# Attention beside a gated dense block: the order of the lead-in, with key projections in half pieces, two query transfers on ScalarE's queue and later weight splits

## The chip, the core and the metric

The kernel runs on one core of a Trainium2 chip. The metric is the device time of one execution in microseconds (us), as a median over several runs. Each engine (TensorE or PE, VectorE or DVE, ScalarE or ACT, GpSimd or POOL, SyncE or SP) takes its own instructions strictly in order and meets the others through semaphores; a DMA transfer is issued from an engine's instruction stream. So the order in which instructions stand on each engine is a large part of what a kernel is.

## What is computed

```
xn = layernorm(x)                                  # x: 2048 x 512
q, k, v = xn @ wq, xn @ wk, xn @ wv                # 32 heads of 16; k and v: one head for all
o = softmax(q k^T / 4) v,   s = o @ wo
h = xn @ w1 + b1,   a = h * tanh(softplus(h))      # 512 -> 1792
out = x + s * silu(a @ w2)
```

## The kernel before

The program is written out completely, engine by engine, by a planner in Python. There are two parts.

**The loop** (lines 1573 to 1620) has 512 steps: 32 groups of query heads ("v", 4 heads of one chunk of 512 rows each; c = chunk) times 16 blocks of 128 keys. A step issues 4 score products e (L1098, of 64 rows of the array each; ScalarE takes the exponential of each, L1100), up to 8 half-height pieces of dense products (`Mm.half`, L120, target `xps`), 4 products m (L1119) whose row maxima VectorE takes (L1123), and 4 products pv of exponentials and values (L1187). The m belong to the next group of heads but one: their maxima, turned and moved into two rows of the query tile, become the exponent's shift. Two half-height products, one in each half of the array, run beside each other. The dense products make groups: 12 for a block of 128 columns of q or of the first dense matrix (m1), 15 or 12 for a block of rows of the second (m2). A group of 15 goes through the loop by fives if the planner sees spare steps when the group begins, else by eights (`begin`, `g.most`).

**The lead-in** (lines 1277 to 1551) computes what the first step needs: statistics and norms of the four chunks of x, their transposition by TensorE (L302, `xp`), the first query projection (12 products), keys and values of all four chunks, and the first 40 pairs of m, a pair being the product for either half of the array and its two maxima. For chunks 1 to 3 the keys and values go four stages: `k_part` (`kq`, 16 products of 32 output rows, L336), a copy by ScalarE (`k_stage`, `vt`), `k_sum` (`kp`, one product, L345), and copies into `ks` by ScalarE (`k_high`, L356) and then VectorE (`k_low`, L239). A pair m_n of head group 0 needs the keys of chunk n/8. Values follow through `vt`, a transposition by TensorE (`vp`, L372) and a copy by VectorE into `vaug` (L375).

The lead-in's order is made by a list scheduler over `Task` objects (engine, planned duration, function, dependencies, a priority). At each turn it takes the option with the earliest planned start. If TensorE has a gap longer than a bound, option "X" puts three dense products into it (`fill(3)`) or a filler (`keep_warm`, target `warm`, L1434); if ScalarE has one, option "J" splits a weight (float32 into a high part by ScalarE, L461, and a low part by GpSimd, L164) or runs a piece of the activation of m1 (`hb`, `t`, `u`). The maxima use three banks of PSUM (six once the last transposition is issued), so a product m waits for the maximum three products earlier. The evacuation of a finished dense group is a task for ScalarE, not before 0.35 us (2.9 us for the first query group) after the group's end (`put_off`).

The first query group's result (`qh`, `ql`) goes into the query tiles of head groups 0 and 1 by 24 transfers of 32 KB (L784), 12 for each, all from SyncE's queue: piece p (pairs m_0 to m_3 need p = 0, m_4 to m_7 p = 1) and half a, each with two copies of `qh` and one of `ql`. `q_dma` makes the tasks for it.

Of the kernel before, what the change touches and what calls it, by code (L numbers as in the profile page):

```python
# [126 lines left out]
def block_kernel(ctx: ExitStack, tc: tile.TileContext, x, wq, wk, wv, wo, w1, b1, w2, out):  # L127
# [200 lines left out]
    kq_of = {}  # L328
    vp_of = {}

    def k_part(c):
        kq = ps_v.tile([P, C], F32, tag="v", name=f"kq{c}")
        for h in range(2):
            z = slice(C // 2 * h, C // 2 * (h + 1))
            for dt in range(NDT):
                pe.matmul(kq[32 * dt:32 * dt + 32, z], wkf[:, dt, P - 32:P], xf_of[c][dt // 2][:, dt % 2, z], start=True, stop=True)  # L336
        kq_of[c] = kq
# [420 lines left out]
    def q_group(c, b):  # L758
        it = item("wq", ("q", b), wq[:, P * b:P * (b + 1)].rearrange("(t p) n -> p t n", p=P))

        def post(ps):
            qh = sb.tile([P, C], F32R, tag="qh", name=f"qh{c}_{b}", bufs=1)
            ql = sb.tile([P, C], F32R, tag="ql", name=f"ql{c}_{b}", bufs=1)
            first = (c, b) == (0, 0)
            if first:
                act.activation(qh, ps, AF.Copy)
                lead["q"](lambda: sub(dve, ql, ps, f(qh)))
            else:
                qf = sb.tile([P, C], F32, tag="qf", name=f"qf{c}_{b}", bufs=1)
                act.activation(qf, ps, AF.Copy)  # L770
                gap[0] += 1
                hi_pool(qh, qf)
                sub(pool, ql, qf, f(qh))
            for k in range(2):
                v = 8 * c + 2 * b + k

                def dmas(v=v, k=k, parts=((0, 0), (0, 1), (1, 0), (1, 1))):
                    q = qt_of[v] = qts[v % 3]
                    for p, a in parts:
                        o = 64 * a  # L780
                        r = 64 * k + 16 * (2 * p + a)
                        for d, src in ((o, qh), (o + 16, qh), (o + 32, ql)):
                            sp_at(0.63)
                            sp.dma_start(f(q[d:d + 16, p]), f(src[r:r + 16]))  # L784
                if first:
                    lead["qdma"](lambda ps, dmas=dmas: dmas(parts=[(p, a) for p in ps for a in range(2)]))
# [538 lines left out]

    def q_dma(fn):
        v = len(qready)
        qready[v] = None

        def move(p):  # L1330
            fn(ps=(p,))
            qready[v] = (qready[v] or ()) + (now[0] + 6 * 0.63 + 2.0,)
        for p in range(2):
            task("SP", 6 * 0.63, lambda p=p: move(p), [lead["qlow"]], prio=1 + p + 2 * v)

    lead["q"], lead["qdma"] = q_low, q_dma

# [28 lines left out]
    for c0, c1 in ((0, 1), (1, 2), (2, 3), (3, 4)):  # L1366
# [4 lines left out]
        for c in range(c0, c1):  # L1371
# [39 lines left out]
            if c == 0:  # L1411
                k0 = kp = task("PE", 0.9, lambda c=c: k_proj(c, (0,)), xs)
                for dt in range(1, 4):
                    kp = task("PE", 0.9, lambda c=c, dt=dt: k_proj(c, (dt,)), [kp], lat=0.0)
            else:
                kq = task("PE", 1.0, lambda c=c: k_part(c), xs)
                kg = task("ACT", 0.6, lambda c=c: k_stage(c), [kq])
                bank("v", 1, kq, [kg])
                k0 = kp = task("PE", 1.0, lambda c=c: k_sum(c), [kg])
# [38 lines left out]
    while True:  # L1458
# [27 lines left out]
        if k == "M":  # L1486
            if MSEQ[m_next[0]] == (0, 8 * NC - 8):
                keep_warm(3)
            for a in range(2):
                m_one(a)  # L1490
            d = max(T["DVE"], s + 0.45)
            m_ends += [d + 0.6, d + 1.2]
            T["DVE"] = d + 1.2
            T["PE"] = s + (0.25 if kind[0] == "M" else 0.45)
            kind[0] = "M"
            if vdone[0] == 0 and min(m_next) >= m_need(0):
                vdone[0] = 1
                r = c_rows(0)
                r1 = task("DVE", 0.85, lambda r=r: (r[0](), r[1](), r[2](), r[3]()), prio=-4)
                rows[:] = [r1]  # L1500

                def move():
                    r[4]()
                    cdone[0] = now[0] + 2 * 0.65 + 2.0
                task("SP", 2.6, move, [r1])
        elif k == "X":
            fresh = cur["g"] is None
            if cur["g"] is not None or not waiting and begun[0] < 1 + (s - 18) / X_US and begin():
                begun[0] += fresh
                fill(3)  # L1510
                T["PE"] = s + 0.23 * 3 + (0.2 if kind[0] == "M" else 0)
                kind[0] = "X"
            else:
                keep_warm()
                T["PE"] = s + 0.25
                kind[0] = "X"
        elif k == "J":
            tag = next((g for g in ("wq", "ws", "wb") if (g == "wq" or s > 19.0) and arrived(g) and busy[0] + E0 < s + 0.5), None)
            n = ran[0]
            if tag:  # L1520
                split(tag)
                T["ACT"] = s + 0.6
            else:
                gap[0] = 0
                if not pool_due():
                    act_jobs(1)
                T["ACT"] = s + (0.65 if ran[0] > n else 0.15)
        else:
            plan[e].remove(k)
            k.fn()  # L1530
            T[e] = max(s, T[e]) + k.us + (0.15 if e == "PE" and kind[0] == "M" else 0)
            k.end = T[e]
            if e == "PE":
                kind[0] = "T"
# [102 lines left out]
```

## Time and profile before

| | |
|---|---|
| median of 3 runs (1576.19 to 1576.45) | 1576.33 us |
| the profiled execution | 1576.55 us |
| its span, first to last instruction | 1574.4 us |
| busy: TensorE, VectorE, ScalarE, GpSimd | 1562.6, 1341.1, 1307.8, 633.7 us |
| granted TensorE clock | 1.0 |
| first m product | 24.73 us after the span's start |
| last maxima of head group 0 done, turning begins (L1154) | 72.31 us |
| first half-height product (the loop's first step) | 77.93 us |
| first pv | 86.26 us |

A row of the timeline has start, length, engine, line, operation, output and inputs, shapes and types, a count of merged instructions, and in brackets how long the engine idled before it and what ended the wait. The chain of waits is followed back from the last instruction: at each point it names what was late. A row of the windows has the stretch, its length, and for each engine the busy time with the number of instructions. TensorE is busy 99% of the span, but ends of products are modelled, so its share does not tell how full it is; in the lead-in one reads VectorE's gaps instead.

### The profile page before, as it was taken

To read this page: it belongs to the slowest core of one execution; us is meant where nothing else is said; L and a number is where in the kernel's file an instruction comes from. 1 tells how busy PE (TensorE), PEld (TensorE's weight loads), DVE (VectorE), ACT (ScalarE), POOL (GpSimd) and SP (SyncE) were. 2 spreads that over 40 slices of the span, in tenths; PEclk is the share of its full clock that TensorE was granted. 3 is DMA by queue.
4 is the path that set the end of the run, shared out by engine and by line. 5 is a ranking of instruction groups with operands and counts; after the bars stand their busy time and mean duration, and the time that the engine had idled before them with its cause. 6 is when DMAs were issued, how large, how long until landed. Compare 5 with 4: busy or idle time off the path is not lost.

```text
span 1574.4 us, 31742 instructions
## 1 busy us (share of the span) xinstructions
PE 1562.6 (99%) x11738; PEld 842.0 (53%) x11738; DVE 1341.1 (85%) x2329; ACT 1307.8 (83%) x2518; POOL 633.7 (40%) x683
## 2 busy tenths in 40 slices
PE   9999999999999999999999999999999999999998
PEld 5555555555555555555555555555555555555554
DVE  8998888889889888888998988888889998888832
ACT  7588788798998779878989887887898878789886
POOL 4774266284464105503515320471251515126412
PEclk9999999999999999999999999999999999999999
DMA  6243231232331314122032222211332213032020
GB/s 191 93 124 112 65 101 44 60 118 84 125 97 41 103 44 137 45 69 83 24 100 65 64 93 69 85 59 30 112 99 85 74 40 111 19 111 58 15 81 28
DMA packets 74666, 124.31 MB, mean 79 GB/s; under 512 B 21520, under 2 KB 35344, under 8 KB 74512
## 3 DMA queue, kind: packets, MB, share of 16 engines
q1 hardware_dynamic: 74512, 122.29, 25.2%
q8 instruction: 93, 1.52, 0.4%
q14 instruction: 61, 0.50, 0.1%
HBM read 74.78 MB, written 26.21 MB: 64 GB/s over the span
## 4 chain that ended last, share of the span: by engine, by line
PE 95%; DVE 4%; ACT 1%; DMA 0%; issue 0%; SPq 0%; ACTq 0%; DVEq 0%
PE xps L120 44%; PE pv L1187 32%; PE e L1098 9%; PE m L1119 7%; DVE mb L1123 3%; PE late L120 1%; PE xps L116 0%; ACT pt L1100 0%; DMA xin<-in_dram 0%; PE late L1098 0%; PE kp L351 0%; PE wop L120 0%; PE xp L302 0%; PE late L116 0%; PE wop L116 0%
## 5 line engine op out<-in xcount | busy, mean ns | idle before, releaser
L1123 DVE TENSOR_REDUCE mb<-m 128x1 f32<-128x512 f32 x2048 | 1274.2, 683 | 171.3 <-PE m L1119 152.3
L1100 ACT ACTIVATE pt<-e 128x512 f32<-128x512 f32 x2018 | 1061.6, 602 | 220.7 <-PE e L1098 212.3
L1119 PE MATMUL m<-ks,qt 48*128 48x512 f32 (+1 forms) x2048 | 829.9, 421 | 1.6 <-DVE ks L239 0.5
L1098 PE MATMUL e<-qt,ks 64*128 64x512 f32 x2018 | 740.4, 401 | 0.3
L1187 PE MATMUL pv<-pt,vaug 128*32 128x512 f32 x4096 | 543.0, 604 | 0.0
L1119 PEld LDWEIGHTS m<-ks,qt 48*128 48x128 f32 (+1 forms) x2048 | 372.9, 185 | 55.7 <-DVE mb L1123 18.5
L1098 PEld LDWEIGHTS e<-qt,ks 64*128 64x128 f32 x2018 | 373.3, 186 | 17.9 <-ACT pt L1100 7.5
L120 PE MATMUL xps<-wbs,act 64*128 64x512 f32 x1248 | 339.1, 408 | 0.2
L120 PEld LDWEIGHTS xps<-wbs,act 64*128 64x128 f32 x1248 | 217.7, 185 | 177.4 <-ACT pt L1100 105.8
L120 PE MATMUL xps<-xt,ws 64*128 64x512 f32 x1104 | 305.8, 410 | 0.1
L120 PEld LDWEIGHTS xps<-xt,ws 64*128 64x128 f32 x1104 | 190.6, 185 | 182.7 <-ACT pt L1100 116.5
L174 POOL TENSOR_SCALAR t<-t 128x512 f32<-128x512 f32 x56 | 34.4, 615 | 395.1 <-ACT t L838 394.9
L1187 PEld LDWEIGHTS pv<-pt,vaug 128*32 128x32 f32 x4096 | 81.9, 108 | 137.4 <-issue 129.1
L164 POOL TENSOR_TENSOR hb<-hb,t 128x512 f32<-128x512 f32 x56 | 72.1, 1287 | 65.6 <-ACT t L851 52.4
L120 PE MATMUL xps<-xt,wq 64*128 64x512 f32 x336 | 93.2, 410 | 0.0
L120 PEld LDWEIGHTS xps<-xt,wq 64*128 64x128 f32 x336 | 58.0, 185 | 55.2 <-ACT pt L1100 35.2
L120 PE MATMUL xps<-wbs,ot_all 64*128 64x512 f32 x288 | 79.5, 409 | 0.0
L120 PEld LDWEIGHTS xps<-wbs,ot_all 64*128 64x128 f32 x288 | 49.6, 185 | 46.7 <-ACT pt L1100 29.3
L164 POOL TENSOR_TENSOR hb<-hb,u 128x512 f32<-128x512 f32 x56 | 72.3, 1291 | 4.4
L164 POOL TENSOR_TENSOR u<-u,t 128x512 f32<-128x512 f32 x56 | 71.8, 1282 | 4.7
L164 POOL TENSOR_TENSOR act<-hb,act 128x512 fp32r<-128x512 f32 x55 | 70.8, 1288 | 4.6
L159 POOL TENSOR_SCALAR qh<-qf 128x512 fp32r<-128x512 f32 x15 | 9.3, 620 | 111.8 <-ACT qf L770 76.2
(158 smaller groups left out, 954.9 us busy)
## 6 DMA issues: line engine op xcount, KB each, us to landing
wbs<-w SPq DMA_DIRECT2D x36, 512.0 KB
ws<-w SPq DMA_DIRECT2D x35, 512.0 KB
qt<-qh SPq DMA_DIRECT2D x256, 32.0 KB
w<-wbs SPq DMA_DIRECT2D x14, 512.0 KB
wq<-wq SPq DMA_DIRECT2D x14, 512.0 KB
wbs<-wo SPq DMA_DIRECT2D x12, 512.0 KB
rawws<-in_dram SPq DMA_DIRECT2D x21, 256.0 KB
rawwb<-in_dram SPq DMA_DIRECT2D x20, 256.0 KB
```

The costliest lines, as they stand in the source:

```text
L120: i = self.pe.matmul(ps, self.lhs()[o], self.rhs()[o], start=(self.k == 0 and self.halves == 0), stop=(self.k == self.tot - 1 and self.hal ...
L159: pool.tensor_scalar(o, i, 1.0, 0.0, op0=ALU.mult, op1=ALU.add)
L164: eng.tensor_tensor(out=o, in0=a, in1=b, op=op)
L174: pool.tensor_scalar(o, o, lim, 0.0, op0=ALU.min, op1=ALU.max)
L1098: pe.matmul(e, ks[o:o + 64, P * k:P * (k + 1)], q[o:o + 64, p], start=True, stop=True)
L1100: r = act.activation(pt, e, AF.Exp, scale=0.25)
L1119: pe.matmul(m, q[o, p, P * t:P * (t + 1)], ks[o, C * kb:C * (kb + 1)], start=True, stop=True)
L1123: r = dve.reduce_max(out=mb_of[v][:, kb, z:z + 1], in_=m, axis=AX.X)
L1187: pe.matmul(o[32 * j:32 * j + 32], vaug[:, k], pt, start=(k == 0), stop=(k == 15))
```

## The change

- `k_part` and `k_sum` take a half h of the 512 columns and become two tasks of 0.5 us each instead of one of 1.0, so other work can stand between the halves.
- `q_dma`: of the six transfers for the first piece of head group 0, the two copies of `qh` for half 1 are issued from ScalarE's queue right behind the copy that makes `qh`; SyncE's task for that piece has four left (planned as 3 x 0.63 us). The planned duration of that ScalarE task grows from 0.69 to 1.95 us.
- The task for `ql` gets priority -4.
- Option X is offered for gaps over 0.15 us instead of 0.35.
- A weight split in option J also waits until GpSimd has no task due (norms of chunks 2 and 3).

```
-    def k_part(c):
-        kq = ps_v.tile([P, C], F32, tag="v", name=f"kq{c}")
-        for h in range(2):
+    def k_part(c, h):
+        if not h:
+            kq_of[c] = ps_v.tile([P, C], F32, tag="v", name=f"kq{c}")
+        kq = kq_of[c]
+        for h in (h,):
...
-    def k_sum(c):
-        kp_of[c] = ps_v.tile([P, C], F32, tag="v", name=f"kp{c}")
-        pe.matmul(kp_of[c], ksum, vt_of[c], start=True, stop=True)
+    def k_sum(c, h):
+        if not h:
+            kp_of[c] = ps_v.tile([P, C], F32, tag="v", name=f"kp{c}")
+        z = slice(C // 2 * h, C // 2 * (h + 1))
+        pe.matmul(kp_of[c][:, z], ksum, vt_of[c][:, z], start=True, stop=True)
...
-                        for d, src in ((o, qh), (o + 16, qh), (o + 32, ql)):
-                            sp_at(0.63)
-                            sp.dma_start(f(q[d:d + 16, p]), f(src[r:r + 16]))
+                        for n in which:
+                            if eng is sp:
+                                sp_at(0.63)
+                            eng.dma_start(f(q[o + 16 * n:o + 16 * n + 16, p]), f((qh, qh, ql)[n][r:r + 16]))
...
-        t = task("ACT", 0.69, fn, at=now[0] + lead.get("late", 0.35))
+        t = task("ACT", 1.95 if "late" in lead else 0.69, fn, at=now[0] + lead.get("late", 0.35))
...
-        lead["qlow"] = task("DVE", 0.69, fn, at=T["ACT"] + 0.7)
+        lead["qlow"] = task("DVE", 0.69, fn, at=T["ACT"] + 0.7, prio=-4)
...
-        def move(p):
-            fn(ps=(p,))
-            qready[v] = (qready[v] or ()) + (now[0] + 6 * 0.63 + 2.0,)
+        def move(p, n):
+            if v or p:
+                fn(parts=[(p, 0), (p, 1)])
+            else:
+                fn(parts=[(p, 0)])
+                fn(parts=[(p, 1)], which=(2,))
+            qready[v] = (qready[v] or ()) + (now[0] + n * 0.63 + 2.0,)
+        if not v:
+            fn(parts=[(0, 1)], which=(0, 1), eng=act)
...
-                kq = task("PE", 1.0, lambda c=c: k_part(c), xs)
+                k0 = task("PE", 0.5, lambda c=c: k_part(c, 0), xs)
+                kq = task("PE", 0.5, lambda c=c: k_part(c, 1), [k0], lat=0.0)
...
-        if e0 is None or e0[0] > T["PE"] + 0.35:
+        if e0 is None or e0[0] > T["PE"] + 0.15:
...
-            tag = next((g for g in ("wq", "ws", "wb") if (g == "wq" or s > 19.0) and arrived(g) and busy[0] + E0 < s + 0.5), None)
+            tag = next((g for g in ("wq", "ws", "wb") if (g == "wq" or s > 19.0) and arrived(g) and busy[0] + E0 < s + 0.5 and not pool_due()), None)
```

Since the scheduler decides by planned times, all of the lead-in's order changes, and the loop's up to step 24; from there on TensorE's order is the same as before. Line numbers after the change are larger by up to 13. Three places follow. In the names, the number after m_ is the half of the array and the next one the pair; numbers at the end of a name count tiles.

TensorE, from the last key product of chunk 0 to the second pair of m. Before:

```order
L351 MATMUL kp_323<-xf_1_279,wkf 128x512 x2
L1434 MATMUL warm<-qt_79 128x512 x3
L116 MATMUL xps<-xt_216,ws_341 128x512 x9
L372 MATMUL vp_391<-ident,vt_368 128x32 x4
L302 MATMUL xp_397<-ident,xin_0_164 128x128 x4
L1119 MATMUL m_0_0_407<-ks,qt_77 128x512
L1119 MATMUL m_1_0_410<-ks,qt_77 128x512
L302 MATMUL xp_417<-ident,xin_1_166 128x128 x4
L1119 MATMUL m_0_1_423<-ks,qt_77 128x512
```

And now:

```order
L354 MATMUL kp_327<-xf_1_279,wkf 128x512 x2
L1447 MATMUL warm<-qt_79 128x512 x7
L1123 MATMUL m_0_0_386<-ks,qt_77 128x512
L1123 MATMUL m_1_0_389<-ks,qt_77 128x512
L1447 MATMUL warm<-qt_79 128x512 x3
L375 MATMUL vp_401<-ident,vt_370 128x32 x4
L1123 MATMUL m_0_1_413<-ks,qt_77 128x512
```

Nine dense products have left this place, the first pair stands ahead of the value transposition vp, and fillers and vp stand between the first and the second pair.

VectorE, around the copy into ks for chunk 1 (mb of two numbers: the maxima of head groups 0 and 1). Before:

```order
L1123 TENSOR_REDUCE mb_406<-m_1_7_535 128x1
L239 SCALAR_TENSOR_TENSOR ks<-ks,ksgn,kp_524 112x512
L1123 TENSOR_REDUCE mb_553<-m_0_0_554 128x1
L1123 TENSOR_REDUCE mb_553<-m_1_0_557 128x1
L1123 TENSOR_REDUCE mb_553<-m_0_1_571 128x1
L1123 TENSOR_REDUCE mb_553<-m_1_1_574 128x1
L375 COPY vaug<-vp_565 128x4x16
L1123 TENSOR_REDUCE mb_406<-m_0_8_593 128x1
```

And now:

```order
L1127 TENSOR_REDUCE mb_385<-m_1_7_531 128x1
L1127 TENSOR_REDUCE mb_539<-m_0_0_540 128x1
L1127 TENSOR_REDUCE mb_539<-m_1_0_543 128x1
L1127 TENSOR_REDUCE mb_539<-m_0_1_556 128x1
L1127 TENSOR_REDUCE mb_539<-m_1_1_559 128x1
L239 SCALAR_TENSOR_TENSOR ks<-ks,ksgn,kp_536 112x512
L1127 TENSOR_REDUCE mb_385<-m_0_8_571 128x1
```

The copy has moved behind the two pairs of head group 1 and directly ahead of m_8, the first pair that needs it. The copy for chunk 2 stands directly ahead of m_16 now, where it stood ahead of m_11; that for chunk 3 stands ahead of m_24 in both.

TensorE in the loop, step 20 up to its last e (xps<-wbs,act: the second dense matrix). Before:

```order
L120 MATMUL xps<-wbs,act_1_833 128x512
L1119 MATMUL m_1_16_1924<-ks,qt_79 128x512
L120 MATMUL xps<-wbs,act_2_1094 128x512
L1098 MATMUL e_0_1928<-qt_78,ks 128x512
L120 MATMUL xps<-wbs,act_2_1094 128x512
L1119 MATMUL m_1_17_1933<-ks,qt_79 128x512
L120 MATMUL xps<-wbs,act_2_1094 128x512
L1098 MATMUL e_1_1937<-qt_78,ks 128x512
L120 MATMUL xps<-wbs,act_3_1311 128x512
L1098 MATMUL e_2_1942<-qt_78,ks 128x512
L1119 MATMUL m_0_16_1946<-ks,qt_79 128x512
L1098 MATMUL e_3_1949<-qt_78,ks 128x512
```

And now, from its second e:

```order
L1102 MATMUL e_1_1942<-qt_78,ks 128x512
L120 MATMUL xps<-wbs,act_1_1046 128x512
L1123 MATMUL m_1_18_1947<-ks,qt_79 128x512
L120 MATMUL xps<-wbs,act_1_1046 128x512
L1102 MATMUL e_2_1951<-qt_78,ks 128x512
L120 MATMUL xps<-wbs,act_2_1219 128x512
L1123 MATMUL m_1_19_1956<-ks,qt_79 128x512
L120 MATMUL xps<-wbs,act_2_1219 128x512
L1102 MATMUL e_3_1960<-qt_78,ks 128x512
```

The step holds eight half-height pieces where it held five. Counted over the order, the lead-in issues 66 dense products where it issued 75, and the loop up to the end of step 23 has 144 halves where it had 126.

More of the change, by code (lines that the diff above doesn't have):

```diff
@@ L336, in k_part @@
                 pe.matmul(kq[32 * dt:32 * dt + 32, z], wkf[:, dt, P - 32:P], xf_of[c][dt // 2][:, dt % 2, z], start=True, stop=True)
-        kq_of[c] = kq
     def k_stage(c):
@@ L775, in post, with dmas @@
                 v = 8 * c + 2 * b + k
-                def dmas(v=v, k=k, parts=((0, 0), (0, 1), (1, 0), (1, 1))):
+                def dmas(v=v, k=k, parts=((0, 0), (0, 1), (1, 0), (1, 1)), which=(0, 1, 2), eng=sp):
                     q = qt_of[v] = qts[v % 3]
@@ L781, in dmas @@
                         r = 64 * k + 16 * (2 * p + a)
-                        for d, src in ((o, qh), (o + 16, qh), (o + 32, ql)):
-                            sp_at(0.63)
-                            sp.dma_start(f(q[d:d + 16, p]), f(src[r:r + 16]))
+                        for n in which:
+                            if eng is sp:
+                                sp_at(0.63)
+                            eng.dma_start(f(q[o + 16 * n:o + 16 * n + 16, p]), f((qh, qh, ql)[n][r:r + 16]))
                 if first:
-                    lead["qdma"](lambda ps, dmas=dmas: dmas(parts=[(p, a) for p in ps for a in range(2)]))
+                    lead["qdma"](dmas)
                 else:
@@ L1328, in q_dma @@
         qready[v] = None
-        def move(p):
-            fn(ps=(p,))
-            qready[v] = (qready[v] or ()) + (now[0] + 6 * 0.63 + 2.0,)
+        def move(p, n):
[7 more added lines that the diff above has]
+            fn(parts=[(0, 1)], which=(0, 1), eng=act)
         for p in range(2):
-            task("SP", 6 * 0.63, lambda p=p: move(p), [lead["qlow"]], prio=1 + p + 2 * v)
+            n = 6 if v or p else 3
+            task("SP", n * 0.63, lambda p=p, n=n: move(p, n), [lead["qlow"]], prio=1 + p + 2 * v)
     lead["q"], lead["qdma"] = q_low, q_dma
```

5 lines of the change are left out of this document (3 added, 2 removed).

## The prediction

> **What bounds the kernel now.** I read the page's span first, then the chain of waits over the first 95 us, then VectorE's timeline there. Where the lead-in ends, the chain reads (start, length, what ended last, number of instructions):
>
> ```profile
> 73.25 12.54 DVE mb L1123 x21
> 85.84 0.49 PE m L1119
> ```
>
> The profiled execution took 1576.55 us, 2.15 around its span of 1574.4, and 0.22 more than the median of 1576.33. Up to 85.84 the chain is VectorE's row maxima (L1123); from there TensorE holds it, step after step. So the change, whose new order ends before step 24 of 512, can gain only where VectorE idles before 85.84, and pays where it leaves TensorE more work after that. VectorE's rows, the idle time ahead of a group in brackets:
>
> ```profile
> 22.86 0.75 DVE L239 SCALAR_TENSOR_TENSOR ks<-ks,ksgn,kp 112x512 fp32r<-112x512 f32 x1
> ...
> 25.26 8.89 DVE L1123 TENSOR_REDUCE mb<-m 128x1 f32<-128x512 f32 x14 [0.71 <-PE m L1119]
> 34.42 1.29 DVE L1123 TENSOR_REDUCE mb<-m 128x1 f32<-128x512 f32 x2 [0.27 <-PE m L1119]
> 35.63 0.74 DVE L239 SCALAR_TENSOR_TENSOR ks<-ks,ksgn,kp 112x512 fp32r<-112x512 f32 x1
> 36.28 2.48 DVE L1123 TENSOR_REDUCE mb<-m 128x1 f32<-128x512 f32 x4
> 38.67 0.22 DVE L375 COPY vaug<-vp 128x64 f32<-128x64 f32 x1
> 38.80 1.28 DVE L1123 TENSOR_REDUCE mb<-m 128x1 f32<-128x512 f32 x2
> 41.33 1.29 DVE L1123 TENSOR_REDUCE mb<-m 128x1 f32<-128x512 f32 x2 [1.24 <-PE m L1119]
> ...
> 47.66 13.58 DVE L1123 TENSOR_REDUCE mb<-m 128x1 f32<-128x512 f32 x22
> 61.16 0.74 DVE L239 SCALAR_TENSOR_TENSOR ks<-ks,ksgn,kp 112x512 fp32r<-112x512 f32 x1
> 62.48 2.48 DVE L1123 TENSOR_REDUCE mb<-m 128x1 f32<-128x512 f32 x4 [0.59 <-PE m L1119]
> ...
> 73.17 14.40 DVE L1123 TENSOR_REDUCE mb<-m 128x1 f32<-128x512 f32 x24
> ```
>
> A run of 24 maxima lasts 14.40, so one pitch is 0.60 and a pair (both halves of the heads) 1.20; a copy into ks takes 0.65 of the queue (35.63 to 36.28), a copy into vaug about 0.14 (38.67 to 38.80). From 25.26 to 62.48 there are 52 maxima, 26 pairs. The waits worth having are the 0.27, the 1.24, another between 41.33 and 47.66 (eight maxima and the copies into ks and vaug need 5.6 of those 6.33), short ones inside the first group, the late start at 25.26, and the 0.59 behind the last ks copy. After 47.66 there is little to win but that last one. A chain that starts earlier gains at 62.48 only what it has not lost by then in new waits.
>
> **The first maximum.** TensorE and the transfers ahead of it:
>
> ```profile
> 20.50 1.26 PE L1434 MATMUL warm<-qt 128*128 128x512 f32 x3
> ...
> 24.73 0.49 PE L1119 MATMUL m<-ks,qt 64*128 64x512 f32 x2
> ```
>
> ```profile
> 18.29 1.24 SPq L784 DMA_DIRECT2D qt<-qh  x2
> ...
> 21.46 0.59 SPq L784 DMA_DIRECT2D qt<-ql  x1
> ...
> 24.54 2.25 SPq L784 DMA_DIRECT2D qt<-qh  x2
> ```
>
> The ks copy ends at 23.61; vp and a transposition stand between it and the first score product at 24.73, whose maximum follows 0.53 later. Now the product stands directly behind seven fillers, which start at 20.50 and take 0.3 to 0.4 each: 23.3 at the latest. It waits for ks alone: issue 23.66, maximum 24.19, **1.07 earlier**. Its six query transfers were all issued by 22.05 and had landed by 24.73, so landing takes at most 2.7. With two of them on ScalarE, SyncE issues its four by about 20.8, landed by 23.5 at the latest. The move to ScalarE therefore buys nothing beyond that; ks would be waited for anyway. On ScalarE nothing showed a DMA issue yet. Bounds: nothing, and the longest here, 2.25 for two. I take 1.2 for two as in SyncE's rows: qh ends at 18.27, so ScalarE is free at 19.5, and the first norm (0.45), one sum (0.7) and the first ks (from 21.17, behind its product) follow without delay. At 2.25 ks would still start by about 21.8, some 0.6 late, and VectorE, busy until 22.86, would see nearly nothing of it.
>
> The Trainium skill, page "DMA: Bandwidth & Descriptors", section "Issuing engines are not separate DMA queues", says that such a move saves only the sequencer's time to issue, since all queues share the same DMA engines. By it the move is worth at most the 1.2 of issue and, with ks later than the transfers, 0 in the sum; the trace has the issue time but shows no transfer from ScalarE.
>
> **From the second pair to the fourth chunk's keys.** The price list for what stands between two pairs:
>
> ```profile
> 35.78 0.73 PE L1434 MATMUL warm<-qt 128*128 128x512 f32 x2
> 36.51 0.41 PE L372 MATMUL vp<-ident,vt 32*128 32x32 f32 x4
> ...
> 39.80 1.07 PE L336 MATMUL kq<-xf,wkf 128*32 128x256 f32 x16
> ...
> 43.10 0.96 PE L116 MATMUL xps<-xt,ws 128*128 128x512 f32 x3
> ```
>
> I take 0.75 for three products (their rows overlap the next pair by 0.2), 0.6 for a transposition, 0.55 for half of kq, as much for half of kp, and 0.43 for a pair. So a pair with one of these beside it fits in about 1.2, and kq and kp in one piece no longer hold VectorE up by 1.24. But the new order puts other things between:
> - Second pair: three fillers, the last of which needs the bank of the first maximum (ends 24.85), then vp: product 25.5, maximum 26.03 where VectorE was free at 25.47. **New wait 0.56.**
> - Nine pairs to the second pair of head group 1, one vaug copy and 0.3 of small lateness (where two transpositions, or a half of kq and one, share a gap): 26.03 + 10.8 + 0.14 + 0.3 = 37.3.
> - The second ks copy now comes after those two pairs, at 37.3 to 37.95, and the next product needs it. Before, the same two pairs stood behind it and hid the way over TensorE. **New wait 0.55** (the 0.59 of 62.48 shows such a one): maximum at 38.5, against 38.80.
> - Then 0.43 + 0.75 + two fillers 0.6 + vp 0.37 ahead of the next product: 40.1, maximum 40.65, **wait 0.8**, where it was 1.24.
> - Seven pairs and a vaug copy: 40.65 + 8.4 + 0.15 = 49.2.
> - The third ks copy follows there, again with the next product behind it. ScalarE's part of it is queued behind the evacuation of the dense group whose last products stand behind the pair m_13 (about 46.2), its exponential and two scalings:
>
> ```profile
> 50.24 0.62 ACT L838 ACTIVATE t<-hb 128x512 f32<-128x512 f32 x1
> 50.77 2.21 ACT L211 ACTIVATE xin<-xin,nbias,rstd 128x512 f32<-128x512 f32 x3
> ```
>
>   With 0.6 + 0.6 + 2 x 0.72 that is 48.85, and the key copy ends at 49.55. **Waits 0.4 and 0.6**: maximum at 50.85, against 51.6 before (47.66 plus three pairs and small waits).
> - Eight pairs, a vaug copy, the fourth ks copy: 61.25. Nine products and three fillers stand ahead of the next pair, so 61.9 to 62.2 against 62.48.
>
> So VectorE wins 1.07 at the start, and keeps **0.3 to 0.6; I take 0.45**. From 62.48 to the end of the 24 maxima nothing changes its length. The earlier norm of the third chunk, splits behind norms and products in shorter gaps cost nothing here because VectorE's chain covers them.
>
> **What is left for the loop.** The lead-in issues 66 products where it issued 75 (the order's rows up to the first half-height product). The loop gets 18 halves more: one more each in steps 0, 1, 12 and 13, two in steps 2 and 3, and in steps 20 to 23 ten more, since a group of the second dense matrix goes there by 8, 8, 7 and 7 where it went by fives. Three stretches of four steps each, cut at the first pv of a step, with the count of halves under PE:
>
> ```profile
> 134.88:146.28 11.40, 5.70 (x20) 3.41 (x20) 1.00 0.59 180
> 146.28:157.66 11.38, 6.65 (x24) 4.14 (x24) 1.00 0.19 51
> 157.66:169.81 12.15, 8.02 (x30) 5.26 (x30) 1.00 0.05 17
> ```
>
> ```profile
> 86.26:89.11 2.85, 1.20 (x4) 0.66 (x4) 1.00 0.77 229
> ```
>
> Steps of four, five and six halves cost the same 2.85 (2.85, 11.40 / 4, 11.38 / 4); thirty in four steps cost 0.75 more than twenty. So the first eight halves are free, the first three steps also lying under VectorE's run, and the last ten cost **0.75**. The splits that moved from ScalarE to GpSimd's queue in the loop (0.6 each) are needed five and more microseconds after they end by GpSimd's own order, so I take 0; without that cover each would cost its own 0.6 to 1.9.
>
> **Sum:** 1576.55 - 0.45 + 0.75 = 1576.85 for the profiled execution; less 0.22 for the median, **1576.6**. Of its own this reckoning is good to 0.8 either way.
>
> **The rivals.**
> - *The new waits are shorter than I reckon.* The waits of 0.56, 0.8 and 0.4 come from TensorE or ScalarE being late by my adding up, each within what the rows leave open. If they are gone, 1.7 more is won: 1574.9. For it speaks that the lead-in before runs gapless from 47.66. The two waits behind ks copies stay in any case.
> - *Every half counts.* From 24 to 30 halves costs 0.77, or 0.128 a half; if all 18 cost that, the loop pays 2.3: 1578.2. Against it stand the equal stretches of 20 and 24. The Trainium skill, page "TensorE: Matmul & The Clock Gate", section "Back-to-back issue gap", gives 0.216 us between matmuls of 512 columns. Halves in pairs would by it make nine such gaps, 1.94 us, and 1577.8; the trace agrees above six halves a step and not below.
> - *Slower: a weight load holds the second ks.* In ScalarE's queue the second query split now stands right ahead of that ks copy. Its raw load is issued at about 28.5 (22.15 before), behind head group 1's first transfers. ScalarE wants it at 34.5 and VectorE the copy 1.45 after it could be had. A load's price:
>
> ```profile
> 57.14 2.79 SPq L514 DMA_DIRECT2D rawws<-in_dram  x2
> ...
> 61.98 0.63 ACT L461 ACTIVATE early<-rawws 128x512 fp32r<-128x512 f32 x1 [1.31 <-DMA rawws<-in_dram]
> ```
>
>   That one was there 2.05 after its issue ended. The mechanism decides from 7 us on, and each further microsecond is a full one; at 10.5 us the time is 1580.
> - *The transfers do not do what they are moved for.* That is in the forecast: ks sets the start.
>
> **How the numbers follow.** Forecast 0.60, first rival 0.22, second 0.13, third 0.05. The range from 1574.8 to 1578.4 takes in the first two rivals and the outer bounds of the waits. Faster by over 0.2% (about what a measurement of this kernel can tell; below 1573.2) would take both the first rival and free halves: 0.04. Slower by over 0.2% (above 1579.5) is the third rival and an unseen price of ScalarE's transfers: 0.06. Between: 0.90.
>
> **What would show it.** Right: the first maximum near 24.2, idle groups of 0.5 to 0.8 behind the second and third ks copies and ahead of the ninth product's second pair, the four-maxima group behind the fourth ks at 61.9 to 62.2, and steps 20 to 23 at 12.15 together. Wrong: a first maximum after 25, gapless maxima from 38 to 60, or steps 0 to 3 longer than 2.9.

## The result, and the profile after

| | before | after |
|---|---|---|
| median (10 runs each) | 1576.34 us | 1579.93 us (1579.50 to 1585.71) |
| the profiled execution | 1576.55 us | 1581.10 us |
| its span, and the time around it | 1574.4, 2.15 | 1579.3, 1.8 |
| maximum of m_24 (first behind the fourth ks copy) | 62.48 | 66.75 |
| first pv | 86.26 | 90.51 |

The change made the kernel slower by 3.6 us: the ratio of the times is 1.0025, 95% interval 1.0017 to 1.0033. The forecast was 0.3 slower, with a range that ended at 1578.4. VectorE's timeline of the profiled execution after, as it was shown for before:

```profile
22.76 0.75 DVE L239 SCALAR_TENSOR_TENSOR ks<-ks,ksgn,kp 112x512 fp32r<-112x512 f32 x1
24.11 1.29 DVE L1127 TENSOR_REDUCE mb<-m 128x1 f32<-128x512 f32 x2 [0.60 <-PE m L1123]
26.45 1.29 DVE L1127 TENSOR_REDUCE mb<-m 128x1 f32<-128x512 f32 x2 [1.05 <-PE m L1123]
...
30.31 4.87 DVE L1127 TENSOR_REDUCE mb<-m 128x1 f32<-128x512 f32 x8 [0.81 <-PE m L1123]
...
40.86 1.29 DVE L1127 TENSOR_REDUCE mb<-m 128x1 f32<-128x512 f32 x2 [0.58 <-PE m L1123]
...
52.97 0.75 DVE L239 SCALAR_TENSOR_TENSOR ks<-ks,ksgn,kp 112x512 fp32r<-112x512 f32 x1 [1.06 <-ACT vt L370]
...
64.86 0.75 DVE L239 SCALAR_TENSOR_TENSOR ks<-ks,ksgn,kp 112x512 fp32r<-112x512 f32 x1 [0.28 <-ACT vt L370]
66.75 2.48 DVE L1127 TENSOR_REDUCE mb<-m 128x1 f32<-128x512 f32 x4 [1.14 <-PE m L1123]
```

The first maximum is at 24.11, where I had put it (24.19). From there nothing holds: m_1 comes at 26.45 (forecast 26.03), m_8 at 40.86 (38.5), and m_24 at 66.75, 4.27 later than before where I had it 0.45 earlier. The windows say what TensorE was doing (start and end, length, busy time and instructions of each engine, and behind POOL the granted clock, then the transfers' share and rate):

```profile
20.00:23.60 3.60, 2.60 (x10) 1.48 (x9) 3.30 (x11) 3.02 (x8) 0.83 (x2) 1.00 0.26 59
23.60:26.10 2.50, 2.43 (x11) 1.33 (x11) 1.29 (x2) 1.74 (x3) 1.75 (x7) 0.99 0.22 52
26.10:29.50 3.40, 3.40 (x15) 2.39 (x14) 2.70 (x5) 1.59 (x4) 0.00 (x0) 0.50 0.23 52
...
38.90:40.30 1.40, 0.00 (x0) 0.00 (x0) 1.37 (x3) 1.40 (x5) 0.00 (x0) 1.00 0.00 0
...
52.70:56.80 4.10, 3.02 (x15) 1.77 (x16) 3.24 (x6) 3.98 (x11) 2.33 (x3) 1.00 0.00 0
56.80:60.20 3.40, 3.40 (x12) 2.37 (x13) 3.02 (x6) 1.82 (x5) 1.75 (x2) 0.50 0.35 143
```

Twice, for 3.4 us each, TensorE ran at half its clock, which no stretch of the lead-in before shows. It had idled within 3 us before each: 1.0 of the 3.6 us ahead of 23.60, and 1.1 of the 4.1 from 52.70. It idled 1.4 at 38.90 too, and no half clock followed. The chain of waits shows the other half of the story:

```profile
22.61 1.00 issue
23.61 0.70 PE m L1123 x2
...
42.97 0.89 PE xps L116 x3
43.85 0.43 PE m L1123 x2
...
48.08 0.91 PE xps L116 x3
49.00 0.70 ACT hb L834
49.72 0.63 ACT t L842
50.35 1.41 ACT xin L211 x2
51.76 0.57 ACT ks L359
52.35 0.60 ACT vt L370
52.97 0.76 DVE ks L239
53.77 0.50 PE m L1123 x2
```

(On ScalarE, hb and t begin the activation of a finished dense group, and xin is the scaling of a chunk of x.) The chain runs over TensorE from 20.98 up to 48.99 with one break of 2.0 (the second pair of head group 1 and the second ks copy), then over ScalarE, then the ks copy. The chain before, over the same stretch:

```profile
27.08 0.61 PE m L1119 x2
...
33.96 0.47 PE m L1119 x2
34.44 1.28 DVE mb L1123 x2
...
51.59 9.65 DVE mb L1123 x16
```

It ran over TensorE too up to 34.44, and only behind that mostly over VectorE's maxima. The prediction took all of it, up to 85.84, for VectorE's. VectorE's timeline hides the difference: the 14 maxima from 25.26 took 8.89 where 14 times 0.60 is 8.4, since each gap was too short for a bracket.

So there are two theories. **C, the clock:** idles of a microsecond halve TensorE's clock, and that is the loss. **W, the waits:** the new order leaves VectorE waiting for TensorE and for late keys, at any clock.

In the loop the forecast held. The halves in steps 20 to 23 after, cut at the first pv of a step, with the count of halves under PE:

```profile
139.00:151.09 12.09, 8.01 (x30) 5.24 (x30) 1.00 0.62 183
```

Thirty halves in 12.09, where I had 12.15. The other steps up to there keep their 2.84 to 2.88. Against before the loop runs 4.25 late at its first pv and 4.9 to 5.0 from step 24 on; 0.35 comes back around the span.

### The profile page after: what moved, and what is told of

The parts are those of the page before. It is cut to its first block, busy times and chain, and to the rows that moved or that the text cites. A ratio compares the mean times of both kernels' runs of the same rounds, so it can differ in the third digit from the quotient of the medians.

```text
span 1579.3 us, 31779 instructions
## 1 busy us (share of the span) xinstructions
PE 1564.0 (99%) x11759; PEld 844.3 (53%) x11759; DVE 1340.3 (85%) x2329; ACT 1307.9 (83%) x2517; POOL 632.6 (40%) x682
## 4 chain that ended last, share of the span: by engine, by line
PE 96%; DVE 2%; ACT 1%; DMA 0%; SPq 0%; issue 0%; ACTq 0%; DVEq 0%
PE xps L120 45%; PE pv L1191 32%; PE e L1102 9%; PE m L1123 7%; DVE mb L1127 2%; PE xps L116 1%; PE late L120 0%; ACT pt L1104 0%; PE xp L302 0%; DMA xin<-in_dram 0%; PE warm L1447 0%; PE kp L354 0%; PE late L1102 0%; PE kq L338 0%; ACT xin L211 0%
## 5 line engine op out<-in xcount | busy, mean ns | idle before, releaser
L1123 PEld LDWEIGHTS m<-ks,qt 48*128 48x128 f32 (+1 forms) x2048 | 372.7, 185 | 57.7 <-DVE mb L1127 15.9
```

The source lines that it names most:

```text
L1123: pe.matmul(m, q[o, p, P * t:P * (t + 1)], ks[o, C * kb:C * (kb + 1)], start=True, stop=True)
```

## The experiments

Fillers first, since they change what TensorE does in its idle time and leave the order of all else. In each table of this part, "m_24 - ks" is the start of m_24's maxima less that of the first copy into ks, both from VectorE's timeline: 39.62 before, 43.99 after. It leaves out when an execution's first data came (in the executions with a figure there, the first ks copy started between 21.87 and 23.11). Dense products of the lead-in are counted up to the first e here and in the expectations, 77 before and 68 after; that is two more each, both of half height, than in the count up to the first half.

### The clock or the waits

**fill_three**, on the changed kernel, where a pair is issued:

```
             if MSEQ[m_next[0]] == (0, 8 * NC - 8):
                 keep_warm(3)
+            if MSEQ[m_next[0]] in {(0, 0): 4, (0, 8): 5, (0, 16): 4}:
+                keep_warm({(0, 0): 4, (0, 8): 5, (0, 16): 4}[MSEQ[m_next[0]]])
```

> The changed kernel with fillers put where TensorE idles for a microsecond in its lead-in: four ahead of m_0, five ahead of m_8, four ahead of m_16; nothing else moves. Theory C (the clock): the idles make the gate halve TensorE's clock for 3.4 us twice, and that is most of the 3.6 us lost; then the granted clock is 1.00 from 8 us on, and the time 1576.8 to 1577.8. Theory W (the waits): the new order's waits of VectorE cost the time by themselves; fillers stand where TensorE waits anyway, so 1579.5 to 1580.1, whatever the clock.

**fill_first** has only `(0, 0): 4` of it.

> The changed kernel with four fillers ahead of m_0 only. Theory C: the half clock between 26 and 29.5 goes and the one between 57 and 60 stays (0.79 in 56 to 64); about half the gain of the three places, 1578.0 to 1578.8. Theory W: unchanged, 1579.5 to 1580.1.

**before_idle**, on the kernel before:

```
-            if MSEQ[m_next[0]] == (0, 8 * NC - 8):
-                keep_warm(3)
```

> The kernel before without the three fillers ahead of m_24, so that TensorE idles 1.2 us there where it idled 0.5; the order of all else stays. Theory C: a stretch of 3.4 us at half clock follows, and the time rises by 0.3 to 1.5 us, to 1576.6 to 1577.8. Theory W: TensorE waits there for the copy into ks either way, clock or no clock the time stays at 1576.3 (0.2 either way).

**undo_pool**, on the changed kernel:

```
-... and busy[0] + E0 < s + 0.5 and not pool_due()), None)
+... and busy[0] + E0 < s + 0.5), None)
```

> The changed kernel with one part undone, the later weight splits: the lead-in has 9 dense products more, three of them behind m_0 and six ahead of m_16. The idle ahead of m_0 stays, that ahead of m_16 is filled. Theory C: the half clock at 26 stays, the one at 57 goes, and the 0.7 us that the loop paid for 18 halves go too: 1577.6 to 1578.4. Theory W: the copies into ks still stand directly ahead of the products that need them, so only the loop's 0.7 goes: 1579.0 to 1579.4.

| | median, us | ratio to before (95%) | half clock in the profiled lead-in | m_24 - ks |
|---|---|---|---|---|
| fill_three | 1579.08 | 1.0015 (1.0006 to 1.0024) | none | 41.81 |
| fill_first | 1579.80 | 1.0024 (1.0014 to 1.0035) | 40.3 to 50.6 | |
| before_idle | 1576.60 | 1.0008 (0.9998 to 1.0018) | none | 39.64 |
| undo_pool | 1583.94 | 1.0039 (1.0027 to 1.0051) | 27.1 to 44.2 | |

With fillers at the three places the half clock is gone from the profiled execution, and VectorE's timeline at full clock stands bare:

```profile
22.73 0.75 DVE L239 SCALAR_TENSOR_TENSOR ks<-ks,ksgn,kp 112x512 fp32r<-112x512 f32 x1
24.07 1.29 DVE L1127 TENSOR_REDUCE mb<-m 128x1 f32<-128x512 f32 x2 [0.60 <-PE m L1123]
26.31 1.29 DVE L1127 TENSOR_REDUCE mb<-m 128x1 f32<-128x512 f32 x2 [0.94 <-PE m L1123]
...
34.30 2.49 DVE L1127 TENSOR_REDUCE mb<-m 128x1 f32<-128x512 f32 x4 [0.38 <-PE m L1123]
37.06 1.29 DVE L1127 TENSOR_REDUCE mb<-m 128x1 f32<-128x512 f32 x2 [0.27 <-PE m L1123]
38.27 0.74 DVE L239 SCALAR_TENSOR_TENSOR ks<-ks,ksgn,kp 112x512 fp32r<-112x512 f32 x1
39.59 1.29 DVE L1127 TENSOR_REDUCE mb<-m 128x1 f32<-128x512 f32 x2 [0.58 <-PE m L1123]
41.74 1.29 DVE L1127 TENSOR_REDUCE mb<-m 128x1 f32<-128x512 f32 x2 [0.86 <-PE m L1123]
...
43.07 7.58 DVE L1127 TENSOR_REDUCE mb<-m 128x1 f32<-128x512 f32 x12
51.71 0.75 DVE L239 SCALAR_TENSOR_TENSOR ks<-ks,ksgn,kp 112x512 fp32r<-112x512 f32 x1 [1.06 <-ACT vt L370]
53.11 2.48 DVE L1127 TENSOR_REDUCE mb<-m 128x1 f32<-128x512 f32 x4 [0.66 <-PE m L1123]
...
64.54 2.48 DVE L1127 TENSOR_REDUCE mb<-m 128x1 f32<-128x512 f32 x4 [0.98 <-PE m L1123]
```

m_24 comes at 64.54, 2.06 later than before, at full clock. Neither theory had it right. Of the 3.6 us, 0.85 go with the fillers (1579.93 to 1579.08; ten of the eleven runs lie below the fastest of the changed kernel). What stays is 2.5 against the runs of before taken beside it (1576.56) and 2.7 against the first ones (1576.34): mostly the waits, and the loop's share. In the profiled execution after, with its two half-clock stretches, the clock cost 2.2 up to m_24 (66.75 against 64.54).

fill_first shows that the clock does not follow the idles one for one. The half clock behind m_0 is gone as C said; a longer one came behind the idle ahead of m_8, which had none in the execution after:

```profile
40.30:50.55 10.25, 10.25 (x40) 4.55 (x38) 5.94 (x11) 3.68 (x11) 2.37 (x7) 0.50 0.41 124
```

That is three times 3.4, and its first pv came 4.06 later than that of fill_three. Its median of 1579.80 lies where W had it, but not for W's reason: four runs with a mean clock of 0.999 took 1578.57 to 1579.80, three with 0.996 or 0.997 took 1581.24 to 1582.63. In undo_pool TensorE stood 2.55 us ahead of m_0, and the half clock that followed lasted five times 3.4:

```profile
27.10:44.20 17.10, 17.10 (x66) 9.03 (x65) 11.73 (x19) 9.90 (x24) 3.69 (x8) 0.50 0.28 97
```

The single runs agree. Two of undo_pool with a mean clock of 1.0 took 1579.77 and 1580.51, four with 0.994 to 0.996 took 1583.17 to 1586.60. Of before_idle's ten runs seven had 0.998 or more and took 1575.75 to 1577.21; three had 0.994 or 0.995 and took 1580.73 to 1582.39. Its median does not tell it from before, and the profiled execution, one of the seven, shows the idle (1.23 ahead of m_24) and no half clock behind it. The kernel before had such runs 4 times in the 93 beside these experiments (0.995 to 0.997, 1579.57 to 1582.87). So three in ten point to the idle, but no trace here shows it doing so in that kernel. C is right that the half clock is a part of the loss and that fillers remove it, and wrong that it is most of it. The fillers fill an idle and add work at once, so these runs do not tell whether the idle itself or the low share of work around it brings the half clock. Both expectations of undo_pool missed: its order at full clock is no better than the changed kernel's, although it has 9 dense products more.

### Which part makes the waits

**keys_first** writes ScalarE's vt of chunk 2 behind VectorE's ks copy; the fillers of fill_three are in all of this group (in undo_q_f without the four ahead of m_0):

```
     def k_low(c):
...
         kready[c] = now[0] + 0.85
+        if late_v:
+            late_v.pop()()
...
     def v_copy(c):
+        if c == 2 and not late_v:
+            late_v.append(lambda: v_copy_(c))
+        else:
+            v_copy_(c)
+
+    def v_copy_(c):
```

> The changed kernel with the fillers of fill_three, and ScalarE's copy vt of chunk 2 written behind VectorE's copy into ks, which then no longer waits for vt (it started 0.03 behind vt's end, at 51.71). If that wait costs what it shows, the third ks copy starts 0.6 earlier, the maximum of m_24 comes at 63.9 to 64.1 instead of 64.54, and the time is 1578.3 to 1578.7 against 1579.08. Rival: TensorE's transpositions and pairs bound the stretch anyway; then m_24 stays at 64.4 to 64.6 and the time at 1579.1.

**undo_half_f:** one task of 1.0 again for both halves of `k_part`, and one for those of `k_sum`.

> The changed kernel with the same fillers and the projections of chunks 1 to 3 whole again; the first pair still comes at 24.1. Theory A (gaps with two pieces in them, half of a projection and a transposition, cost 0.3 each, and the halves made them): m_24's maximum at 63.5 to 64.2 and the time 1578.0 to 1578.8. Theory B (the early first pair and what it pushes behind itself cost the time, the halves are innocent): m_24 at 64.5 to 65.5 since whole pieces bring their waits of 1 back, time 1579 to 1580.

**undo_x_f:**

```
-        if e0 is None or e0[0] > T["PE"] + 0.15:
+        if e0 is None or e0[0] > T["PE"] + 0.35:
```

> The changed kernel with the same fillers and the bound for dense products at 0.35 again; 62 dense products in the lead-in instead of 68, three of them ahead of m_16. Theory A: same pieces beside each other, m_24 within 0.3 of 64.54, and six products or twelve halves more for the loop: 1579.1 to 1579.9. If dense products in short gaps are what delays VectorE: m_24 at 63.5 to 64.2, 1578.4 to 1579.

**undo_q_f:** the two transfers back on SyncE (`n = 6`, 0.69 for the evacuation).

> The changed kernel with fillers ahead of m_8 and m_16, and all query transfers on SyncE's queue again. The value transposition and the first four transpositions of chunk 1 stand ahead of m_0 again, so the first maximum comes near 25.3. Theory A: the gaps are mixed otherwise and the halves stay, m_24 within 0.4 of 64.54 and the time 1578.7 to 1579.5. Theory B (the early first pair is bought by putting vp and eight transpositions between the first pairs): the chain has caught up by m_4, m_24 comes 0.5 to 1 earlier, 63.5 to 64.0, and the time is 1578.0 to 1578.6.

| | median, us | ratio to before (95%) | m_24 - ks | profiled half clock |
|---|---|---|---|---|
| keys_first | 1579.08 | 1.0017 (1.0007 to 1.0026) | 42.14 | none |
| undo_half_f | 1583.98 | 1.0045 (1.0030 to 1.0060) | 40.89 | 62.8 to 66.3 |
| undo_x_f | 1579.62 | 1.0022 (1.0012 to 1.0031) | 40.33 | none |
| undo_q_f | 1586.04 | 1.0071 (1.0046 to 1.0095) | 40.41 | 63.5 to 66.9 |

In keys_first the third copy started 0.64 earlier (51.07) and nothing came of it by m_24: the pair behind it gained 0.32 (52.79 against 53.11), since the fillers ahead of m_16 now held it up, and by the fourth copy that was lost too. The rival had the time right. The trace shows the wait for vt; that the lateness moved along ScalarE's queue, where vt, the transposed chunk 3 and its norms now stand behind the copy, is argued and not tested by itself.

undo_x_f took 1.5 off the way to m_24, most of the 2.2 that fill_three has over before. Its time did not fall. With its 62 products the loop has had 24 halves more than before by step 24, and from the first pv to there it lost 1.9 against before, 1.3 against fill_three. Behind step 24 it lost another 1.2 against fill_three: the order of its last groups is another too, and the execution ends 15.9 behind the last pv instead of 14.0.

undo_half_f and undo_q_f were 0.9 and 1.4 earlier at m_24 than fill_three. So undoing any one of the three parts gives back 0.9 to 1.5 of the 2.2 there: the parts share that loss, and their shares do not add up. But TensorE idled 1.9 and 2.0 ahead of m_24 in these two and ran at half clock around and behind it, and later in the lead-in VectorE stood 1.23 in both (80.31 and 80.15), behind three dense products that had waited 0.78 for ScalarE's hb in undo_half_f. From the first pv to step 24 they lost 2.4 and 3.7 against before, and undo_q_f ends 15.9 behind its last pv as well. Their times were missed by 4 and 6.5 us.

### Parts alone

On the kernel before (in all three the key sum is two products of 256 columns): **alone_x** has only the bound of 0.15, **alone_half** only the half pieces, **alone_pool** only `and not pool_due()`.

> The kernel before with one part of the change alone: dense products in gaps over 0.15 us instead of 0.35. The lead-in issues five dense products more than before, the keys of chunk 2 come one pair later (kp ahead of m_11). If dense products in short gaps only use idle time: m_24 at 62.5 as before, and ten halves less for the loop at about 0.04 to 0.1 each: 1575.4 to 1576.0. If they push VectorE's chain back by what they last: m_24 at 63.5 or later, time 1576.6 to 1577.6.

> The kernel before with the half pieces alone; seven dense products fewer in the lead-in, the keys of chunk 2 ahead of m_13 and m_14 instead of m_10. If halves remove waits as meant (the 1.24 at 41.33 and the 0.59 at 43.21): m_24 at 61.5 to 62.0 and, with fourteen halves more in the loop, 1576.2 to 1577.0. If late keys and mixed gaps eat it: m_24 at 62.5 to 63.5 and 1577.0 to 1578.2.

> The kernel before with the later weight splits alone: twelve dense products fewer in the lead-in, since the weights are not split yet, eleven fillers ahead of the first pair. If only the count of products matters: 24 halves more for the loop at 0.04 to 0.1 each, 1577.3 to 1578.7, with m_24 at 62.0 to 62.6. If the loop takes them for nothing: 1576.0 to 1576.5.

| | median, us | ratio to before (95%) | m_24 - ks | dense products in the lead-in, to before |
|---|---|---|---|---|
| alone_x | 1581.71 | 1.0034 (1.0022 to 1.0047) | 43.46 | +5 |
| alone_half | 1578.89 | 1.0017 (1.0006 to 1.0028) | 41.37 | -7 |
| alone_pool | 1576.88 | 0.9999 (0.9990 to 1.0008) | 38.84 | -12 |

The lower bound alone costs 5.2, more than the whole change, with a mean clock of 0.999 or 1.0 in all runs. Its VectorE ahead of m_24:

```profile
63.69 0.75 DVE L239 SCALAR_TENSOR_TENSOR ks<-ks,ksgn,kp 112x512 fp32r<-112x512 f32 x1 [1.29 <-ACT vt L370]
66.29 1.29 DVE L1127 TENSOR_REDUCE mb<-m 128x1 f32<-128x512 f32 x2 [1.85 <-PE m L1123]
```

Three products stand ahead of chunk 3's kp there and three more behind it; the keys come late, and then the pair waits behind the products. The half pieces alone cost little at full clock (1576.34 and 1577.07 in its two runs of clock 1.0) and 1 to 9 us where the clock fell (eight runs of 0.992 to 0.998, 1577.52 to 1585.83): TensorE idles 1.45 ahead of m_8 in it. The later splits alone are the one part whose lead-in is faster, by 0.8 at m_24. Their 24 halves cost the loop 1.4 (step 24 against the first pv), so the time is the same.

### One group of three products

In the changed kernel two groups of three dense products stand between vp and kq of chunk 2 in successive gaps, ahead of m_10 and m_11; with the bound undone, one. **x_not10** (with the fillers) moves just that:

```
-        if e0 is None or e0[0] > T["PE"] + 0.15:
+        if e0 is None or e0[0] > T["PE"] + (0.15 if m_next[0] != 13 else 0.35):
```

> The changed kernel with the fillers of fill_three, and the bound for dense products 0.35 at one place only, between m_10 and m_11. There the three products give way to the first half of kq of chunk 2, so kq, kp and with them the third ks copy stand one pair earlier; they come back ahead of m_16, and the lead-in's count stays 68. Theory D (three dense products in a short gap push the next chunk's keys one pair back, and ScalarE's and VectorE's copies of them are then what m_16 waits for): the third ks copy starts 0.8 to 1.2 earlier against the first maximum, m_24 0.5 to 1.2 earlier, the time 1578.0 to 1578.6 against 1579.08. Theory S (ScalarE's queue ahead of the key copy is the bound there, as when the key copy was put ahead of vt): no change, 1579.1.

**x_after** (changed kernel, fillers) and **none_after** (kernel before) have `0.15 if 3 in kready else 0.35`.

> The changed kernel with the fillers, and the bound 0.15 only once the keys of chunk 3 are there, else 0.35; 65 dense products in the lead-in, six ahead less than 68 but three more behind kp of chunk 3. Theory D: VectorE's chain as with the bound undone, m_24 39.0 to 39.4 behind the first maximum (40.5 in fill_three), and the loop pays 0.04 to 0.08 for each of 24 halves: 1578.4 to 1579.4. If the lead-in's order is innocent: 1579.1 or more.

> The kernel before with the bound 0.15 only once the keys of chunk 3 are there: all the same up to kp of chunk 3, then three dense products more ahead of m_24 and three more ahead of a later pair. Theory D: no key waits for them, so m_24 moves by the 0.2 that three products last over the idle of 0.53, and six halves leave the loop: 1576.0 to 1576.6, nothing or a little better than before. If short gaps cost wherever they are: 1577 or more.

| | median, us | ratio to before (95%) | m_24 - ks | first pv to step 24, against before |
|---|---|---|---|---|
| fill_three | 1579.08 | 1.0015 (1.0006 to 1.0024) | 41.81 | +0.6 |
| x_not10 | 1580.15 | 1.0024 (1.0015 to 1.0033) | 41.21 | +2.4 |
| x_after | 1578.67 | 1.0015 (1.0006 to 1.0024) | 40.87 | +1.4 |
| none_after | 1577.28 | 1.0003 (0.9994 to 1.0012) | 39.70 | +1.0 |

TensorE in fill_three, from the second group of products to the second half of kp:

```profile
42.96 0.96 PE L116 MATMUL xps<-xt,ws 128*128 128x512 f32 x3
...
44.28 0.64 PE L338 MATMUL kq<-xf,wkf 128*32 128x256 f32 x8
...
49.34 0.70 PE L348 MATMUL kp<-vt,wkv 128*128 128x256 f32 x2
```

and in x_not10:

```profile
43.17 0.64 PE L338 MATMUL kq<-xf,wkf 128*32 128x256 f32 x8 [0.28 <-DVE vaug L378]
...
48.04 0.70 PE L348 MATMUL kp<-vt,wkv 128*128 128x256 f32 x2
```

The third ks copy of x_not10, in VectorE's timeline:

```profile
50.46 0.74 DVE L239 SCALAR_TENSOR_TENSOR ks<-ks,ksgn,kp 112x512 fp32r<-112x512 f32 x1
```

and ScalarE's rows there:

```profile
48.78 0.69 ACT L359 ACTIVATE ks<-kp,kone 112x512 fp32r<-112x512 f32 x1 [0.67 <-PE kp L348]
...
52.75 0.68 ACT L834 ACTIVATE hb<-xps,b1c 128x512 f32<-128x512 f32 x1
```

Without that one group the last half of kp stands 1.30 earlier (48.04 against 49.34), one pair's time; VectorE's copy waits for nothing any more and starts 1.25 earlier; m_24 comes 0.6 earlier (41.21 against 41.81). So theory D has the chain as it forecast it: with the products in the short gap, the next chunk's keys come a pair later. But the run moves a second thing. In fill_three the dense group to which these products belong ends in time for its hb and t (1.33 together, from 47.74) to stand ahead of the key copy on ScalarE, which starts at 50.50, 0.46 behind kp's end. In x_not10 that group ends later, its hb comes at 52.75, and the key copy waits for kp alone. So how much of the 1.25 is the products themselves and how much their group's evacuation stays open.

The same bound once all keys are there costs m_24 nearly nothing in the kernel before (none_after, 39.70 against 39.62). In the changed kernel it costs 0.54: x_after, which differs from undo_x_f by the bound behind the last keys, has nine products ahead of m_24 where undo_x_f has six, and 40.87 against 40.33. That x_after is still the faster of the two in time (1578.67 against 1579.62) comes from the loop and what follows it. The time of x_not10 was missed by 1.55, upwards, and its loop tells why (steps 14, 15 to 18 and 19 to 22, halves under PE):

```profile
119.03:121.73 2.70, 0.00 (x0) 0.00 (x0) 1.00 0.02 2
121.73:134.32 12.59, 8.03 (x30) 5.25 (x30) 1.00 0.36 127
134.32:146.49 12.17, 8.05 (x31) 5.24 (x30) 1.00 0.55 169
```

A step without any half lasts 2.70, 0.15 less than one of six; four steps with thirty last 12.2 to 12.6 instead of 11.4. The planner let step 14 go empty and sent three groups through by 8, 8, 7 and 7. Halves that merely shift cost nothing up to six in a step, and 0.75 to 1.2 per group of thirty beyond; an empty step pays back nearly nothing. none_after loses its 0.9 that way too, though it has six halves fewer to place; its time came where the rival of theory D had put it (1577 or more), its m_24 where theory D had.

No version here beats the kernel before. alone_pool cannot be told from it.

## Why the prediction was wrong

Point by point, the executions at full clock (fill_three) being the measure of the sum:

1. *VectorE's maxima bound the lead-in, and it gains where they wait less.* Right for before only behind 34.44: up to there the chain before ran over TensorE, and "up to 85.84 the chain is VectorE's row maxima" was a misreading. It is wrong as a frame for after: the chain there runs over TensorE for most of the way to 48.99, and in fill_three to 47.72. I checked each gap against VectorE's 1.20 a pair, but in a row of gaps that take TensorE 1.3 the lateness adds up.
2. *First maximum 24.19, transfers on ScalarE worth nothing more.* 24.11. ScalarE's two issues took 1.22, as taken:

```profile
18.21 1.22 ACTq L788 DMA_DIRECT2D qt<-qh  x2
```

   VectorE's ks copy started 0.1 earlier than before. That fits the rule of the Trainium skill, page "DMA: Bandwidth & Descriptors", section "Issuing engines are not separate DMA queues", by which such a move saves only the time to issue. That the early pair was no gain follows from point 3.
3. **The step that failed: "VectorE wins 1.07 at the start, and keeps 0.3 to 0.6".** At full clock it lost 2.06, a difference of 2.5 from the forecast, in these terms of the sum: the second pair 0.28 late (26.31 for 26.03); nine pairs to m_8 0.8 more (39.59 for 38.5), where I allowed 0.3 of small lateness and the gaps with two pieces took 0.38, 0.27 and several tenths; seven pairs to m_15 0.36 more, since three products and a pair take 0.89 + 0.43 = 1.32 in the chain and not 0.75 + 0.43; the third ks copy 0.66 more and its pair 0.15, since it started 0.03 behind vt, which I had left out of the wait (in keys_first, without that wait, m_24 came no earlier); behind the fourth ks copy 0.3 more. The wait of 0.55 ahead of m_8 and that of 0.8 ahead of m_9 were right: 0.58 and 0.86.
4. *"Products in shorter gaps cost nothing here because VectorE's chain covers them."* Wrong, and a large part of point 3: undone, the bound gives back 1.5 of the 2.2 at m_24; alone it costs 3.8 there. With these products the keys of chunk 2 came later, and nine of them ahead of m_24 held that pair itself. It is not the only root: the transfers undone give back 1.4 and the halves 0.9.
5. **What I did not reckon: the clock.** I quoted 1.0 as granted and took it for given, while forecasting three waits of TensorE near a microsecond. It cost 0.85 in the median and 2.2 in the profiled execution. The Trainium skill, page "TensorE: Matmul & The Clock Gate", section "What's actually happening", has a window of 3413 ns that runs freely; the stretches here (3.4, 10.25 and 17.1) are one, three and five of them, and that it runs freely would fit that the same idle is followed by a half clock in one execution and not in another. The Trainium skill's section "Why this matters for your kernels" on the same page warns of gaps above about 3 us. The measurement differs: half clocks followed gaps of 1.0 to 2.6 us here.
6. *Loop: 0.75 for steps 20 to 23, nothing for the first eight halves.* 12.09 for 12.15; right.
7. *Rivals.* "Every half counts" is refuted by steps of 0 halves in 2.70 and of 4 to 6 in about 2.85; the weight load did not come late to the second ks in any way that the chain shows; shorter waits were the opposite of what came. None of the three had the mechanism.

The sum as it should have been for the median: 2.06 in the lead-in, 0.6 to 0.7 in the loop, -0.35 around the span, 0.85 for the clock, 3.2 to 3.3 against 3.6 measured. What stays open: why the time around the span is 1.8 in the changed kernel and most variants and 2.1 in before, before_idle, undo_x_f and undo_q_f; and which idles bring a half clock. undo_half_f's loss in the loop is the planner's usual share: 2.4 by step 24, as in x_not10, with the same empty step and the same groups by 8, 8, 7 and 7. undo_q_f lost 3.7, and part of the rest can be read from its trace: several of its early steps of six halves last 3.04 to 3.12, and in one of them (93.95 to 96.0) the last m and the last e run one behind the other, 0.23 each, where in the changed kernel they run side by side. Why the planner ordered them so stays open.

## What to carry to other kernels

Before work goes into an engine's idle slots, follow what is queued behind those slots: a key projection that slips by one slot can hold every copy and pair behind it, while the gain of the work that took the slot shows up elsewhere or, in steps below their floor, nowhere. When an order is predicted, add up each engine's time through the whole stretch, not gap by gap against the engine that bounds it now. And wherever a change leaves TensorE waiting a microsecond, count the clock as a term, or put fillers there.

## What the runs showed of the hardware

- Half-clock stretches of TensorE lasted 3.4, 10.25 and 17.1 us. Of eight up to the first pv of the profiled executions, seven began 0.1 to 3.0 us after the end of an idle of TensorE (1.01 and 1.07 in after, 1.45 in fill_first, 2.55 in undo_pool, 1.45 in alone_half, 1.87 in undo_half_f, 2.04 in undo_q_f); the one in alone_pool, at 80.0, in the loop's first steps, followed none above 0.4. Idles of 1.44 (after, ahead of m_8), 1.07 (fill_first, ahead of m_16) and 1.23 (before_idle) were followed by none.
- Fillers in an idle TensorE (five ahead of m_8) cost nothing visible in fill_three, and no half clock followed; in keys_first, where the idle had shrunk, the five ahead of m_16 held the pair up by 0.4 (m_16's product at 52.26, the copy ended at 51.82).
